# 64-row score tiles with the other head's queries zero, and a first group projected straight to padded form

## Chip, cores, metric

One core of a Trainium2 chip. The metric is the time of one launch on the device in microseconds (us). Time before the change: 1094.29 us, median of 3 runs (1092.95 to 1100.68). A trace's span, from first to last instruction, is some 2 to 7 us shorter than such a median.

PE is the matmul engine, PEld its weight load, ACT the scalar engine, DVE the vector engine, POOL and SP the other two; here SP mostly issues DMAs. "SPq" in a trace is SP's queue of instructions. The granted clock is the share of PE's full clock that the trace records: in these traces 1 or 0.5 at any moment (37 stretches of each in the trace before the change), and something between as a mean.

## The reference

Two branches over the same `x` (2048 x 512, bf16), mixed by a gate:

```python
g = sigmoid((x * gate_w).sum(-1, keepdims=True))
a = mha(x, wqkv, wo)          # 32 heads of width 16, softmax over 2048 keys
b = (silu(x @ w_gate) * (x @ w_up)) @ w_down      # F = 1792
return g * a + (1 - g) * b
```

Attention makes 32 x 2048 x 2048 scores, each of which needs an exponential. That is most of the work outside PE.

## The kernel before

The unit of work is a **slot**: one group of four heads (`g`), one block of 512 queries (`qb`), one tile of 128 keys (`kt`). There are 4 x 8 x 16 = 512 slots. In each, four score matmuls produce 128 x 512 scores each, and four PV matmuls (exponentials times values) consume their exponentials five slots later. Between them a pacer inserts pieces of all the other work (projections, gate, FFN, output projection), earliest deadline first. Each engine is given its instructions in program order, and in these traces an instruction that waits holds up those behind it on its engine: at a block boundary of the changed kernel DVE stood idle for 7.12 us before one reciprocal, then ran the next step, which had nothing left to wait for, right behind it.

A head is 16 wide, plus one row for a bound that keeps the exponent small. Each head is given a strip of 32 rows of the PE array:

```python
def score(ps, b):                       # b counts heads over all slots
    n, j = b // 4, b % 4
    ...
    mm(ps, lhsT=kaug[32 * j:32 * j + 32, g, kt * P:(kt + 1) * P],
       rhs=get_qaug(qb)[32 * j:32 * j + 32, g, :], start=True, stop=True, tile_position=(32 * j, 0))
```

Two heads at a time go to ACT (`act_pair`, `s_t` of 1024 columns, two PSUM buffers). Every eighth head (`on_vector`) goes to DVE, which computes its exponential with a polynomial in steps (score tile `d_t`, one PSUM buffer; below this is the "vector bank"):

```python
def on_vector(b):
    return b % 16 in (11, 15) and b < 4 * (SLOTS - 12)
```

Projected K and Q arrive with 16 rows per head; DMAs spread them to the strips, one DMA for each head:

```python
def spread_heads(t, b, src, c0, c1, first_on=None):
    for h in range(8):
        g, j = 2 * b + h // 4, h % 4
        eng = nc.sync if first_on is None or h % 2 == 0 else first_on
        eng.dma_start(out=t[32 * j + 1:32 * j + 1 + DH, g, c0:c1], in_=src[DH * h:DH * (h + 1), 0:c1 - c0])
```

The source of K is one of two staging tiles (`kst`). At the end of a query block the softmax denominators go out to DRAM and back; DVE inverts them, and they are broadcast (`rb`) for the output projection.

```python
def recip(qb, g1):
    ...
    nc.sync.dma_start(out=dn[0:4 * n, :], in_=dds[qb][0:n, :]. ...)
    def spread():
        recip16(rn[0:4 * n, :], dn[0:4 * n, :])          # DVE, in its program order
        ...                                               # to DRAM and broadcast to rb
    vops.append(spread)                                   # within the next slots
```

## Time and profile before

| | before |
|---|---|
| median of runs | 1094.29 us |
| span of the profiled run | 1087.0 us |
| mean granted TensorE clock | 0.833 |
| busy: PE, ACT, DVE | 81%, 81%, 74% |
| first exponential starts | 44.4 us |
| starts of exponentials 1 and 99 apart | 136.2 us |
| the next 782 exponentials | 860.2 us (1.100 each) |
| from there to the end | 46.2 us |

The last four rows come from the starts of the `e_t` instructions in the trace. They cut the span into parts that can be compared between kernels. The prediction below shows the profile's lines.

### The profile page before, as it was taken

How to read it: one execution, taken by the hardware profiler on the slowest of the kernel's cores; microseconds unless marked ns; L12 is line 12 of the kernel's file. 1: busy time of each engine (PE TensorE's matmuls, PEld its weight loads, DVE VectorE, ACT ScalarE, POOL GpSimd, SP SyncE). 2: the span in 40 equal slices, each digit the busy share in tenths (PEclk: the TensorE clock that was granted, in tenths of full speed). 3: DMA queues.
4: the chain of work that ended last, by engine and by line, in shares of the span. 5: the costliest groups of instructions: out<-in, count | busy, mean ns of one | idle time of the engine just before them, and what ended most of it. 6: DMA issues, size and time to landing. Idle time of an engine off the chain costs nothing.

```text
span 1087.0 us, 14674 instructions
## 1 busy us (share of the span) xinstructions
PE 875.1 (81%) x5109; PEld 208.7 (19%) x5109; DVE 807.2 (74%) x1475; ACT 883.2 (81%) x967; POOL 23.2 (2%) x25
## 2 busy tenths in 40 slices
PE   2796588988887888888887788988888788888874
PEld 0121122121221122122221121112221122222210
DVE  2387577787877788779777887778777787887833
ACT  0485577898987799889987898889897799999963
POOL 8000000000000000000000000000000000000000
PEclk9798665798987899689888897779895799889756
DMA  9000100111100001111001111110001011000000
GB/s 256 22 7 23 27 23 24 29 42 36 24 22 26 18 27 43 32 30 38 10 3 39 32 33 37 23 35 18 3 19 49 23 36 31 8 3 4 4 22 20
DMA packets 89774, 32.61 MB, mean 30 GB/s; under 512 B 75944, under 2 KB 89188, under 8 KB 89700
## 3 DMA queue, kind: packets, MB, share of 16 engines
q1 hardware_dynamic: 85012, 27.35, 10.3%
q10 hardware_dynamic: 4560, 4.26, 1.2%
q8 instruction: 40, 0.66, 0.2%
q14 instruction: 34, 0.28, 0.1%
q0 software_dynamic: 128, 0.07, 0.0%
HBM read 20.84 MB, written 2.35 MB: 21 GB/s over the span
## 4 chain that ended last, share of the span: by engine, by line
PE 35%; ACT 25%; DVE 18%; issue 13%; SPq 5%; DMA 3%; ACTq 0%; DVEq 0%
ACT e_t L171 24%; PE s_t L168 9%; PE o_ps L168 8%; DVE u_t L177 6%; DVE y_t L177 5%; PE d_t L168 4%; PE dps L168 4%; PE up L168 3%; PE gp L168 2%; SPq L255 2%; SPq L184 2%; DVE z_t L177 1%; ACT th L171 1%; DMA kaug<-kst 1%; PE a_ps L168 1%
## 5 line engine op out<-in xcount | busy, mean ns | idle before, releaser
L171 ACT ACTIVATE e_t<-s_t 128x1024 bf16<-128x1024 f32 x899 | 855.0, 1032 | 144.1 <-PE s_t L168 136.9
L168 PE MATMUL s_t<-qaug,kaug 32*128 32x512 bf16 x1798 | 371.5, 438 | 112.5 <-ACT e_t L171 108.5
L177 DVE TENSOR_SCALAR y_t<-d_t 128x512 uint16<-128x512 f32 x250 | 171.8, 687 | 115.9 <-PE s_t L168 96.2
L168 PE MATMUL o_ps<-e_t,vaug 128*32 128x512 bf16 x1798 | 231.1, 451 | 4.3 <-ACT e_t L171 4.3
L168 PEld LDWEIGHTS <-kaug 32*128 32x128 bf16 x2048 | 93.7, 93 | 500.5 <-issue 497.2
L177 DVE TENSOR_TENSOR u_t<-u_t,z_t 128x1024 f16<-128x1024 f16 x250 | 173.1, 693 | 8.6
L168 PE MATMUL d_t<-qaug,kaug 32*128 32x512 bf16 x250 | 110.1, 440 | 25.4 <-DVE y_t L177 25.0
L168 PE MATMUL o_ps<-y_t,vaug 128*32 128x512 bf16 x250 | 113.1, 452 | 2.6 <-DVE y_t L177 2.5
L177 DVE TENSOR_TENSOR y_t<-y_t,u_t 128x1024 uint16<-128x1024 uint16 x125 | 86.4, 692 | 4.3
L168 PE MATMUL gp<-xT,wg 128*128 128x512 bf16 x224 | 79.9, 444 | 3.1 <-DVE gs L177 3.1
L168 PE MATMUL up<-xT,wu 128*128 128x512 bf16 x224 | 81.6, 454 | 0.0
L168 PEld LDWEIGHTS <-vaug 128*32 128x32 bf16 x2048 | 51.7, 96 | 149.8 <-issue 149.8
L168 PE MATMUL dps<-wd_t,mt 128*128 128x512 bf16 x224 | 75.7, 428 | 0.0
L177 DVE TENSOR_SCALAR u_t<-z_t 128x1024 f16<-128x1024 uint16 x125 | 53.4, 427 | 4.3
L177 DVE TENSOR_SCALAR z_t<-y_t 128x1024 uint16<-128x1024 uint16 x125 | 53.3, 427 | 4.2
L177 DVE TENSOR_SCALAR y_t<-y_t 128x1024 uint16<-128x1024 uint16 x125 | 53.0, 424 | 2.7
L177 DVE TENSOR_SCALAR u_t<-u_t 128x1024 f16<-128x1024 f16 x125 | 52.7, 422 | 1.9
L177 DVE SCALAR_TENSOR_TENSOR mt<-gs,up 128x512 bf16<-128x512 bf16 x56 | 38.2, 683 | 18.4 <-PE up L168 18.2
L168 PE MATMUL kp<-xT,wqk 128*128 128x512 bf16 x64 | 23.6, 471 | 21.7 <-DMA xT<-in_A_x_dram 21.6
L177 DVE SCALAR_TENSOR_TENSOR gs<-th,gp 128x512 bf16<-128x512 bf16 x56 | 38.1, 680 | 1.5 <-ACT th L171 1.4
L171 ACT ACTIVATE th<-gp 128x512 bf16<-128x512 f32 x56 | 33.9, 605 | 4.5 <-PE gp L168 4.5
L168 PE MATMUL a_ps<-wo_t,on_qb 128*128 128x512 bf16 x64 | 24.8, 462 | 15.7 <-DVE on_qb L177 15.6
(57 smaller groups left out, 273.3 us busy)
## 6 DMA issues: line engine op xcount, KB each, us to landing
wg<-in_B_w_gate_dram SPq DMA_DIRECT2D x56, 128.0 KB
wu<-in_B_w_up_dram SPq DMA_DIRECT2D x56, 128.0 KB
out_dram<-o_t SPq DMA_DIRECT2D x16, 128.0 KB
qaug<-qst SPq DMA_DIRECT2D x124, 16.0 KB
on_qb<-osb SPq DMA_DIRECT2D x124, 16.0 KB
rb<-rr SPq DMA_DIRECT2D x15, 128.0 KB
wd_t<-in_B_w_down_dram ACTq DMA_DIRECT2D x1, 1792.0 KB
kaug<-kst SPq DMA_DIRECT2D x112, 16.0 KB
```

The source lines that it names most:

```text
L168: ordered(nc.tensor.matmul(*args, **kw))
L171: ordered(nc.scalar.activation(*args, **kw))
L177: return lambda *a, **kw: ordered(f(*a, **kw))
L184: nc.sync.dma_start_transpose(out=xT[:, dc, :], in_=x[:, dc * P:(dc + 1) * P])
L255: eng.dma_start(out=t[32 * j + 1:32 * j + 1 + DH, g, c0:c1], in_=src[DH * h:DH * (h + 1), 0:c1 - c0])
```

## The change

Intent: raise the part of the PE array that a score matmul uses, in the hope of a higher granted clock, and start the exponentials sooner. Two heads now share a 64-row tile; the queries of the other head are zero there, so its keys add nothing. Queries are therefore stored twice as wide (`j % 2`), in two buffers for two groups each instead of two for eight. The first group of the first block is projected with weights already padded to strips, which needs no spreading. Loads of `wo`, `w_down` and the gate move from the front to SP behind the transposes of `x`; all head DMAs are on SP; K and Q get new deadlines; each pair of groups has its own bound.

```diff
@@ score
+    HEADS = (0, 2, 1, 3)
     def score(ps, b):
-        n, j = b // 4, b % 4
+        n, j = b // 4, HEADS[b % 4]
-        mm(ps, lhsT=kaug[32 * j:32 * j + 32, g, kt * P:(kt + 1) * P],
-           rhs=get_qaug(qb)[32 * j:32 * j + 32, g, :], ..., tile_position=(32 * j, 0))
+        if qb == 0 and g == 0:
+            ...                                  # 32 rows of q0, the padded first group
+        else:
+            r = slice(64 * (j // 2), 64 * (j // 2) + 64)
+            mm(ps, lhsT=kaug[r, g, kt * P:(kt + 1) * P], rhs=get_qx(qb, g // 2)[r, j % 2, g % 2, :],
+               start=True, stop=True, tile_position=(64 * (j // 2), 0))
@@ on_vector
-        return b % 16 in (11, 15) and b < 4 * (SLOTS - 12)
+        return b % 16 in (10, 15) and 4 * KT <= b < 4 * (SLOTS - 12)
@@ start  (cut)
+    for dc in range(DC):                         # as each quarter of xT arrives
+        for tb in range(QB):
+            mm(kp0[...], lhsT=wpad[1][:, dc, :], rhs=xT[:, dc, ...], ...)
+        mm(qp0[:, :], lhsT=wpad[0][:, dc, :], rhs=xT[:, dc, 0:QBW], ...)
@@ spreading
-            eng = nc.sync if first_on is None or h % 2 == 0 else first_on
+                nc.sync.dma_start(...)           # all on SP; likewise qx<-qst
@@ pacing of K and Q  (cut)
-            prev = [pace.add(k_pieces(b, tb), 0, d - 12 + tb, prev)]
-        qs = [pace.add(q_pieces(qb, b), d - G * KT, d - 100 + 22 * b) for b in range(NB)]
+                    prev = [pace.add(k_pieces(b, tb), 0, d - (9 if first else 22) + tb, prev)]
+            q = pace.add(q_pieces(qb, b), 0 if first else max(0, d - 2 * KT + 1), d - (7 if first else 16))
```

More of the change, by code (lines that the diff above doesn't have):

```diff
@@ L185 @@
     wqk = big.tile([P, DC, 2 * D], BF16, name="wqk")
-    nc.scalar.dma_start(out=wqk[:], in_=A_wqkv[:, 0:2 * D].rearrange("(dc p) c -> p dc c", p=P))
+    for c0 in (0, D):
+        nc.scalar.dma_start(out=wqk[:, :, c0:c0 + 64],
+                            in_=A_wqkv[:, c0:c0 + 64].rearrange("(dc p) c -> p dc c", p=P))
+    for c0 in (0, D):
+        nc.scalar.dma_start(out=wqk[:, :, c0 + 64:c0 + D],
+                            in_=A_wqkv[:, c0 + 64:c0 + D].rearrange("(dc p) c -> p dc c", p=P))
     rb = big.tile([P, NB, QBW], BF16, name="rb")
@@ L191, with late_loads @@
     gw_col = const.tile([P, DC], BF16, name="gw_col")
-    nc.scalar.dma_start(out=gw_col[:], in_=gate_w.rearrange("(dc p) -> p dc", p=P))
     wo_t = big.tile([P, NB, D], BF16, name="wo_t")
-    nc.scalar.dma_start(out=wo_t[:], in_=A_wo.rearrange("(b p) d -> p b d", p=P))
     wo_l = big.tile([P, D], BF16, name="wo_l")
-    nc.gpsimd.memset(wo_l[:], 0.0)
-    for j in range(4):
-        nc.gpsimd.dma_start(out=wo_l[32 * j + 1:32 * j + 1 + DH, :],
-                            in_=A_wo[(H - 4 + j) * DH:(H - 3 + j) * DH, :])
-    wd_t = big.tile([P, FC, D], BF16, name="wd_t")
-    nc.scalar.dma_start(out=wd_t[:], in_=B_w_down.rearrange("(fc p) d -> p fc d", p=P))
-    kaug = big.tile([P, G, S], BF16, name="kaug")
-    for g in range(G):
-        (nc.vector if g < 2 else nc.gpsimd).memset(kaug[:, g, :], 1.0)
+    wd_t = big.tile([P, FC, D], BF16, name="wd_t")
+    def late_loads():
+        nc.sync.dma_start(out=gw_col[:], in_=gate_w.rearrange("(dc p) -> p dc", p=P))
+        nc.sync.dma_start(out=wo_t[:], in_=A_wo.rearrange("(b p) d -> p b d", p=P))
+        for j in range(4):
+            nc.sync.dma_start(out=wo_l[32 * j + 1:32 * j + 1 + DH, :],
+                              in_=A_wo[(H - 4 + j) * DH:(H - 3 + j) * DH, :])
+        nc.sync.dma_start(out=wd_t[:], in_=B_w_down.rearrange("(fc p) d -> p fc d", p=P))
+    kaug = big.tile([P, G, S], BF16, name="kaug")
+    wpad = [big.tile([P, DC, P], BF16, name=f"wpad{i}") for i in range(2)]
+    for i in range(2):
+        nc.vector.memset(wpad[i][:], 0.0)
+    onescol = const.tile([P, 1], F32, name="onescol")
+    nc.vector.memset(onescol[:], 0.0)
+    for j in range(4):
+        nc.vector.memset(onescol[32 * j:32 * j + 1, :], 1.0)
+    bsel0 = const.tile([P, P], BF16, name="bsel0")
+    nc.vector.memset(bsel0[:], 0.0)
+    for j in range(4):
+        nc.vector.memset(bsel0[32 * j:32 * j + 32, 32 * j:32 * j + 1], -1.0)
+    for i in range(2):
+        nc.vector.tensor_copy(
+            out=wpad[i][:, :, :].rearrange("p dc (j c) -> p dc j c", c=32)[:, :, :, 1:1 + DH],
+            in_=wqk[:, :, i * D:i * D + 64].rearrange("p dc (j c) -> p dc j c", c=DH))
+    for g in range(1, G):
+        nc.gpsimd.memset(kaug[:, g, :], 1.0)
     vaug = big.tile([P, KT, G * 4 * VC + 16], BF16, name="vaug")
@@ L215 @@
                    allow_small_or_imprecise_dtypes=True)
-    bsel = const.tile([P, NB, H], BF16, name="bsel")
-    lo_t = const.tile([P, H], F32, name="lo_t")
-    for b in range(NB):
-        for h in range(H):
-            c = 8 * (h % 4) + h // 4
-            if b == 0:
-                nc.vector.memset(lo_t[:, c:c + 1], float(DH * h))
-        ge_t = work.tile([P, H], F32, tag="ge_t", name="ge_t")
-        lt_t = work.tile([P, H], F32, tag="lt_t", name="lt_t")
-        nc.vector.tensor_scalar(out=ge_t[:], in0=lo_t[:], scalar1=pidx[:, 0:1], scalar2=float(P * b),
-                                op0=ALU.subtract, op1=ALU.subtract)
-        nc.vector.tensor_scalar(out=lt_t[:], in0=ge_t[:], scalar1=-float(DH) + 0.5, scalar2=-1.0,
-                                op0=ALU.is_gt, op1=ALU.mult)
-        nc.vector.scalar_tensor_tensor(out=bsel[:, b, :], in0=ge_t[:], scalar=0.5, in1=lt_t[:],
-                                       op0=ALU.is_lt, op1=ALU.mult)
+    bsel = const.tile([P, 8], BF16, name="bsel")
+    lo_t = const.tile([P, 8], F32, name="lo_t")
+    for h in range(8):
+        c = 2 * (h % 4) + h // 4
+        nc.gpsimd.memset(lo_t[:, c:c + 1], float(DH * h))
+    far_t = const.tile([P, 8], F32, name="far_t")
+    nc.vector.tensor_scalar(out=lo_t[:], in0=lo_t[:], scalar1=pidx[:, 0:1], scalar2=None, op0=ALU.subtract)
+    nc.vector.tensor_scalar(out=far_t[:], in0=lo_t[:], scalar1=-float(DH) + 0.5, scalar2=-1.0,
+                            op0=ALU.is_gt, op1=ALU.mult)
+    nc.vector.scalar_tensor_tensor(out=bsel[:, :], in0=lo_t[:], scalar=0.5, in1=far_t[:],
+                                   op0=ALU.is_lt, op1=ALU.mult)
+    nc.gpsimd.memset(wo_l[:], 0.0)
     sbc_t = const.tile([P, P], BF16, name="sbc_t")
@@ L238 @@
     kb = const.tile([P, NB], F32, name="kb")
-    kneg = const.tile([P, NB, H], BF16, name="kneg")
+    kneg = const.tile([P, NB, 8], BF16, name="kneg")
     gval = const.tile([P, KT], F32, name="gval")
@@ L248, with spread_heads @@
     kparts = {}
-    def spread_heads(t, b, src, c0, c1, first_on=None):
+    def spread_heads(t, b, src, c0, c1):
         for h in range(8):
             g, j = 2 * b + h // 4, h % 4
-            eng = nc.sync if first_on is None or h % 2 == 0 else first_on
-            eng.dma_start(out=t[32 * j + 1:32 * j + 1 + DH, g, c0:c1], in_=src[DH * h:DH * (h + 1), 0:c1 - c0])
+            if g > 0:
+                nc.sync.dma_start(out=t[32 * j + 1:32 * j + 1 + DH, g, c0:c1], in_=src[DH * h:DH * (h + 1), 0:c1 - c0])
     def k_pieces(b, tb, act_evac=False):
@@ L273, in f @@
                         vec.tensor_copy(out=seg, in_=st["p"][:, :])
-                    spread_heads(kaug, b, seg, tb * QBW, (tb + 1) * QBW, nc.scalar if b == 0 else None)
+                    spread_heads(kaug, b, seg, tb * QBW, (tb + 1) * QBW)
                     if tb == 0:
@@ L283, in k_bound @@
         vec.tensor_reduce(out=kb[:, b:b + 1], in_=kparts[b][:, :], axis=AX.X, op=ALU.max)
-        vec.tensor_scalar(out=kneg[:, b, :], in0=bsel[:, b, :], scalar1=kb[:, b:b + 1],
+        vec.tensor_scalar(out=kneg[:, b, :], in0=bsel[:, :], scalar1=kb[:, b:b + 1],
                           scalar2=None, op0=ALU.mult)
@@ L305, in v_pieces, with get_qx @@
         return [(2, pc(0)), (2, pc(1))]
-    qaugs = [big.tile([P, G, QBW], BF16, name=f"qaug{i}") for i in range(2)]
-    for t in qaugs:
+    qx = [big.tile([P, 2, 2, QBW], BF16, name=f"qx{i}") for i in range(2)]
+    for t in qx:
         nc.gpsimd.memset(t[:], 0.0)
+    q0 = big.tile([P, QBW], BF16, name="q0")
     aqs = {}
-    def get_qaug(qb):
-        return qaugs[qb % 2]
+    def get_qx(qb, b):
+        return qx[(qb * NB + b) % 2]
     def q_pieces(qb, b, act_evac=False):
@@ L331, in f @@
                         vec.tensor_copy(out=qst[:, :], in_=st["p"][:, :])
-                    qa = get_qaug(qb)
-                    spread_heads(qa, b, qst, 0, QBW, nc.scalar if act_evac else None)
+                    t = get_qx(qb, b)
+                    for hh in range(8):
+                        gg, j = hh // 4, hh % 4
+                        if (qb, b, gg) != (0, 0, 0):
+                            nc.sync.dma_start(out=t[32 * j + 1:32 * j + 1 + DH, j % 2, gg, :],
+                                              in_=qst[DH * hh:DH * (hh + 1), :])
                     aq = work.tile([P, QBW], BF16, tag="aq", name="aq", bufs=4)
@@ L339, in q_pieces, with bound_pieces @@
         return [(2, pc(0)), (2, pc(1))]
-    def bound_pieces(qb, b0, b1):
+    def bound_pieces(qb, b):
         def f():
             bp = ps_m.tile([P, QBW], F32, tag="m", name="bp")
-            for b in range(b0, b1):
-                mm(bp[0:H, :], lhsT=kneg[:, b, :], rhs=aqs[(qb, b)][:, :], start=(b == b0), stop=(b == b1 - 1))
-            bq = work.tile([H, QBW], BF16, tag="bq", name="bq")
-            vec.tensor_copy(out=bq[:, :], in_=bp[0:H, :])
-            qa = get_qaug(qb)
+            mm(bp[0:8, :], lhsT=kneg[:, b, :], rhs=aqs[(qb, b)][:, :], start=True, stop=True)
+            bq = work.tile([8, QBW], BF16, tag="bq", name="bq")
+            vec.tensor_copy(out=bq[:, :], in_=bp[0:8, :])
+            t = get_qx(qb, b)
             for j in range(4):
-                nc.sync.dma_start(out=qa[32 * j:32 * j + 1, 2 * b0:2 * b1, :],
-                                  in_=bq[8 * j + 2 * b0:8 * j + 2 * b1, :])
-        return [(b1 - b0, f)]
+                nc.sync.dma_start(out=t[32 * j:32 * j + 1, j % 2, :, :], in_=bq[2 * j:2 * j + 2, :])
+        return [(1, f)]
     def gate_pieces(t0):
@@ L430 @@
     unready = set()
+    HEADS = (0, 2, 1, 3)
     def score(ps, b):
-        n, j = b // 4, b % 4
+        n, j = b // 4, HEADS[b % 4]
         qb, g, kt = n // (G * KT), (n // KT) % G, n % KT
-        mm(ps, lhsT=kaug[32 * j:32 * j + 32, g, kt * P:(kt + 1) * P],
-           rhs=get_qaug(qb)[32 * j:32 * j + 32, g, :], start=True, stop=True, tile_position=(32 * j, 0))
+        if qb == 0 and g == 0:
+            r = slice(32 * j, 32 * j + 32)
+            mm(ps, lhsT=kaug[r, g, kt * P:(kt + 1) * P], rhs=q0[r, :], start=True, stop=True,
+               tile_position=(32 * j, 0))
+        else:
+            r = slice(64 * (j // 2), 64 * (j // 2) + 64)
+            mm(ps, lhsT=kaug[r, g, kt * P:(kt + 1) * P], rhs=get_qx(qb, g // 2)[r, j % 2, g % 2, :],
+               start=True, stop=True, tile_position=(64 * (j // 2), 0))
     def act_pair(bs):
@@ L488, in pv @@
             c0 = (4 * g + j) * VC
-            assert 4 * n + j not in unready
-            mm(o_of[un][32 * j:32 * j + 32, :], lhsT=vaug[:, kt, c0:c0 + 32], rhs=e_of.pop(4 * n + j),
+            b = 4 * n + HEADS.index(j)
+            assert b not in unready
+            mm(o_of[un][32 * j:32 * j + 32, :], lhsT=vaug[:, kt, c0:c0 + 32], rhs=e_of.pop(b),
                start=(kt == 0), stop=(kt == KT - 1), tile_position=(0, 32 * j), skip_group_check=True)
@@ L551, in f @@
                     if g1 < G and not acc:
-                        acc.append(get_qaug(qb - 1)[:, :, :].rearrange("p g c -> p (g c)").bitcast(F32)
-                                   .rearrange("p (t d) -> p t d", t=TQ))
+                        acc.append(big.tile([P, TQ, D], F32, name="acc"))
                 for b in (2 * i, 2 * i + 1):
@@ L570, in fin_pieces @@
         return [(2, pc(i)) for i in range(2)]
-    for tb in range(QB):
-        for _, f in k_pieces(0, tb, act_evac=(tb % 2 == 0)):
-            f()
-    for _, f in q_pieces(0, 0, act_evac=True):
-        f()
-    V0 = 4
-    for tt in range(2):
-        for _, f in v_pieces(tt, act_evac=True):
-            f()
-    k_bound(0)
-    for _, f in bound_pieces(0, 0, 1):
-        f()
-    for tt in range(2, V0):
+    kp0 = [ps_s.tile([P, 2 * QBW], F32, tag="s", name="kp0") for _ in range(2)]
+    qp0 = ps_m.tile([P, QBW], F32, tag="m", name="qp0")
+    for dc in range(DC):
+        for tb in range(QB):
+            mm(kp0[tb // 2][:, (tb % 2) * QBW:(tb % 2 + 1) * QBW], lhsT=wpad[1][:, dc, :],
+               rhs=xT[:, dc, tb * QBW:(tb + 1) * QBW], start=(dc == 0), stop=(dc == DC - 1))
+        mm(qp0[:, :], lhsT=wpad[0][:, dc, :], rhs=xT[:, dc, 0:QBW], start=(dc == 0), stop=(dc == DC - 1))
+    kpart0 = const.tile([P, 2], F32, name="kpart0")
+    act(out=kaug[:, 0, 0:2 * QBW], in_=kp0[0][:, :], func=ACT.Identity, bias=onescol[:, 0:1], scale=1.0)
+    vec.tensor_scalar(out=kaug[:, 0, 2 * QBW:4 * QBW], in0=kp0[1][:, :], scalar1=onescol[:, 0:1], scalar2=None,
+                      op0=ALU.add)
+    act(out=q0[:, :], in_=qp0[:, :], func=ACT.Copy)
+    vec.tensor_reduce(out=kpart0[:, 0:1], in_=kaug[:, 0, 2 * QBW:4 * QBW], axis=AX.X, op=ALU.max,
+                      apply_absolute_value=True)
+    vec.tensor_reduce(out=kpart0[:, 1:2], in_=kaug[:, 0, 0:2 * QBW], axis=AX.X, op=ALU.max,
+                      apply_absolute_value=True)
+    aq0 = work.tile([P, QBW], BF16, tag="aq", name="aq0", bufs=4)
+    vec.tensor_scalar(out=aq0[:, :].bitcast(U16), in0=q0[:, :].bitcast(U16), scalar1=0x7FFF, scalar2=None,
+                      op0=ALU.bitwise_and)
+    kb0 = const.tile([P, 1], F32, name="kb0")
+    kneg0 = const.tile([P, P], BF16, name="kneg0")
+    vec.tensor_reduce(out=kb0[:], in_=kpart0[:, :], axis=AX.X, op=ALU.max)
+    vec.tensor_scalar(out=kneg0[:], in0=bsel0[:], scalar1=kb0[:, 0:1], scalar2=None, op0=ALU.mult)
+    V0 = 5
+    for tt in range(V0):
+        if tt == 3:
+            bp0 = ps_d.tile([P, QBW], F32, tag="d", name="bp0")
+            mm(bp0[:, :], lhsT=kneg0[:, :], rhs=aq0[:, :], start=True, stop=True)
+            vec.tensor_tensor(out=q0[:, :], in0=q0[:, :], in1=bp0[:, :], op=ALU.add)
         for _, f in v_pieces(tt, act_evac=True):
@@ L595, with bnd @@
     prev = []
-    for b in range(1, NB):
-        d = 2 * b * KT
-        ks = []
-        for tb in range(QB):
-            prev = [pace.add(k_pieces(b, tb), 0, d - 12 + tb, prev)]
-            ks += prev
-        q = pace.add(q_pieces(0, b), 0, d - 7)
-        def bnd(b=b):
-            k_bound(b)
-        kbc = pace.add([(0.5, bnd)], 0, d - 7, ks)
-        prev = [kbc]
-        bc = pace.add(bound_pieces(0, b, b + 1), 0, d - 6, [q, kbc])
-        need.setdefault(d - 3, []).append(bc)
-    for qb in range(1, QB):
-        d = qb * G * KT
-        qs = [pace.add(q_pieces(qb, b), d - G * KT, d - 100 + 22 * b) for b in range(NB)]
-        bc = pace.add(bound_pieces(qb, 0, NB), d - G * KT, d - 10, qs)
-        need.setdefault(d - 4, []).append(bc)
-    gates = [pace.add(gate_pieces(4 * i), 0, 80 + 8 * i) for i in range(4)]
+    for qb in range(QB):
+        for b in range(NB):
+            d = (qb * G + 2 * b) * KT
+            first = qb == 0 and b == 0
+            if first:
+                d = KT
+            after = []
+            if qb == 0:
+                ks = []
+                for tb in range(QB):
+                    prev = [pace.add(k_pieces(b, tb), 0, d - (9 if first else 22) + tb, prev)]
+                    ks += prev
+                def bnd(b=b):
+                    k_bound(b)
+                after = prev = [pace.add([(0.2, bnd)], 0, d - (6 if first else 17), ks)]
+            q = pace.add(q_pieces(qb, b), 0 if first else max(0, d - 2 * KT + 1), d - (7 if first else 16))
+            bc = pace.add(bound_pieces(qb, b), 0 if first else max(0, d - 2 * KT + 1), d - (5 if first else 14), [q] + after)
+            need.setdefault(d - (4 if first else 6), []).append(bc)
+    gates = [pace.add(gate_pieces(4 * i), 40, 80 + 8 * i) for i in range(4)]
     gu = {(qb, fc): gu_chain(qb, fc) for qb in range(QB) for fc in range(FC)}
@@ L637 @@
             pcs = [(pcs[0][0], first)] + pcs[1:]
-            c = pace.add(pcs, 0, a0 + per * 0.6 * (fc + 1) / FC, prev)
+            c = pace.add(pcs, 24, a0 + per * (0.6 if qb < QB - 1 else 0.68) * (fc + 1) / FC, prev)
             prev = [c]
         for tq in range(TQ):
-            c = pace.add(down_pieces(qb, tq), 0, a0 + per * (0.6 + 0.3 * (tq + 1) / TQ), prev + fin_prev)
+            c = pace.add(down_pieces(qb, tq), 0, a0 + per * (0.6 + 0.3 * (tq + 1) / TQ if qb < QB - 1 else 0.68 + 0.32 * (tq + 1) / TQ), prev + fin_prev)
             prev = [c]
@@ L669 @@
             c.force()
+        if n == 8:
+            late_loads()
         pace.begin_slot(n)
```

## The prediction

> **What bounds the kernel now.** I read the page's slices first, then busy time by engine in stretches of 30 us, then the chain of waits, then the timeline of the start.
>
> ```profile
> span 1087.0 us, 14674 instructions
> ...
> PE 875.1 (81%) x5109; PEld 208.7 (19%) x5109; DVE 807.2 (74%) x1475; ACT 883.2 (81%) x967; POOL 23.2 (2%) x25
> ...
> PEclk9798665798987899689888897779895799889756
> ...
> L171 ACT ACTIVATE e_t<-s_t 128x1024 bf16<-128x1024 f32 x899 | 855.0, 1032 | 144.1 <-PE s_t L168 136.9
> L168 PE MATMUL s_t<-qaug,kaug 32*128 32x512 bf16 x1798 | 371.5, 438 | 112.5 <-ACT e_t L171 108.5
> ```
>
> No engine is full over the whole span: ACT (the exponentials e_t) and PE are both at 81%, and ACT's idle time is nearly all waiting for score tiles. The clock row is the odd one: the granted TensorE clock wanders between 0.5 and 1. Stretches of equal length show what it does (columns: stretch, length, PE, PEld, DVE, ACT, POOL busy with counts, clock, DMA share, GB/s):
>
> ```profile
> 480.00:510.00 30.00, 25.71 (x173) 6.82 (x171) 26.97 (x49) 29.80 (x35) 0.00 (x0) 1.00 0.15 34
> ...
> 660.00:690.00 30.00, 28.07 (x137) 5.31 (x136) 22.27 (x41) 24.75 (x28) 0.00 (x0) 0.61 0.13 30
> ...
> 1020.00:1050.00 30.00, 21.92 (x115) 4.46 (x114) 18.29 (x33) 23.97 (x26) 0.00 (x0) 0.53 0.06 19
> ```
>
> At clock 1.00 ACT is the bound (29.80 of 30 us, 35 instructions). At 0.61 PE is the bound (28.07 of 30) and only 28 get through. So the kernel alternates between two bounds, and the clock chooses.
>
> What chooses the clock? The trace's clock records have only the values 0.5 and 1, and every change falls on a grid of 3.413 us. I cut the matmul records of the trace on that grid and weighted each by the part of the array it uses: 1 for a 128x128 matmul, 1/4 for a score tile (32 rows), 1/4 for a PV tile (32 columns). If a window's sum was 6.5 or more, the next window ran at full clock in 145 of 146 cases; below 5 in 1 of 56; between, in about half. Plain busy time does not separate them (660 to 690 is 94% busy and slow). So what keeps the clock up is array area, not time. Mean sums per window: 7.5 in 480:510 (30 full, 70 score, 72 PV matmuls in 30 us), 5.9 in 660:690, 4.0 where attention runs alone (1020 to 1040). Attention tiles alone can't hold the clock; interleaved FFN matmuls do.
>
> Pace, from the starts of the 782 exponentials between 180 and 1040 us: 0.999 us each at full clock (607.6 us / 608), 1.451 at half clock (252.4 / 174). ACT's own floor at full clock is 0.917 from exponential to exponential plus 0.478 for each of 56 tanh, so 0.917 + 0.030 = 0.947.
>
> The start:
>
> ```profile
> 12.55 0.59 PE L168 MATMUL kp<-xT,wqk 128*128 128x512 bf16 x1 [12.55 <-DMA xT<-in_A_x_dram]
> ...
> 23.31 1.01 PE L168 MATMUL kp<-xT,wqk 128*128 128x512 bf16 x2 [1.50 <-DMA xT<-in_A_x_dram]
> ```
>
> The last quarter of xT arrives at 23.3, the first exponential starts at 44.4: 21 us of projections, copies, spreading DMAs and the bound. Between 45 and 180 us only 98 exponentials run in 135 us, with the chain naming kaug spreads and the bound's vector work.
>
> [...] The trace shows 32-row tiles used mostly in pairs: two take 0.39 us at full clock, four 0.60. [...] xT crawled (about 140 KB per 2 us) while the weight loads ran, then moved 430 to 470 KB per 2 us.
>
> **The change part by part.**
> 1. 64-row score tiles. Every score tile outside the first group of the first query block doubles its area, 1/4 to 1/2, at the same 512 columns. Work isn't added in time: 32-row and full matmuls last alike in the groups (438 ns against 454 for up). The sum of 480:510 becomes 7.5 + 70/4 * 3.413/30 = 9.4; attention alone at ACT's pace (about 8.4 scores and 8.4 PV per window) becomes 4.2 + 2.1 = 6.3, in the band that mostly holds; with any FFN matmul it is above. Of 112 windows at half clock, 70 would reach 6.5 with scores at 1/2 even before they speed up. So the clock stays near 1 between about 50 us and the last FFN work. The tail of FFN is also stretched to slot 500 to cover the end.
> 2. Pairs are reordered to heads (0,2),(1,3), so a pair still sits in two different row halves and overlaps. What is lost is four-way overlap, and d_t beside a pair: about 0.21 us for each of 242 d_t tiles, 51 us of PE over the span. PE at full clock is 25.7 of 30, so it becomes about 27.3: still under ACT.
> 3. Vector engine takes 242 score tiles instead of 250. ACT gets 4 exponentials more (+3.7 us). DVE loses 8 * 2.58 = 21 us (0.687 + half of the seven-step chain of 3.78), 6 us of set-up, and gains about 8 us of copies of smaller bounds: 807 to about 788.
> 4. wo and w_down (2.3 MB) leave the first 23 us: at the 236 GB/s of the first 30 us that is 10 us of transfer, of which I count 7.5: last xT at about 16. Then 5 cold matmuls (2.1), a copy of 1024 columns (1.2), two maxima (2.4), the small bound steps (0.7), the bound's matmul and addition (1.3) and V projections beside them: first exponential at about 28 instead of 44.4. The spreading DMAs and their waits fall out for group 0.
> 5. K and Q of the next groups get earlier deadlines (22 slots ahead instead of 12), gates and FFN wait till slots 40 and 24. In the first 16 slots 84 full matmuls (0.27 each in pairs of 0.54, 22.7 us) join 16 * 0.97 us of attention: 38 us for 32 exponentials; then 66 at 1.05 make 69. Together 107 instead of 136.
>
> Sum: first exponential 28, first 98 exponentials 107, then 903 - 98 - 19 = 786 at 0.99 (between floor and the measured full-clock pace, nearer to the latter) = 778, the last stretch 47 as before (19 exponentials, with its wait for the denominators' round trip through DRAM). 960 us as a profiled span; times the ratio of median to span, 1094.3/1087.0, 966 us.
>
> **The rivals.**
> - [...] For it: half of each moving tile is zero, and no run yet has shown how zeros count. Against it: nothing in the records separates windows better than area. Then the clock stays near 0.83 and only parts 4 and 5 pay: about 1050.
> - PE becomes the bound through lost overlap (part 2) [...]
> - DVE becomes the bound. 788 us of work against about 900 us from first exponential to last is 87%; in 480:510 it already runs at 90% beside a full ACT, so it fits, but with little room; a pace of 1.03 gives about 1000.
> - The start stalls: all spreading DMAs are now on one queue (0.59 us per issue), and only two staging buffers for K exist. Some 10 to 15 us.
>
> **Range and chances.** The central sum is 966. A pace near the floor (0.955) takes 27 us off and a shorter tail a few more: 932. Half clock in a sixth of the steady part (131 exponentials * 0.45 = 59 us) or a DVE-bound pace brings about 1005. Even the first rival is faster by over 2%. Faster 0.97, within 2% 0.02, slower 0.01.
>
> **What would show it.** Clock row near 1 from slice 2 to the last but two; mean clock above 0.93 (now 0.833). ACT's idle time before e_t down from 144 to about 60 us; pace per exponential 0.95 to 1.0. First exponential between 26 and 32 us. Score matmuls at full clock still about 0.39 us. The prediction is wrong if the clock still drops during FFN stretches (area idea false), or if it stays at 1 and ACT still waits over 100 us for s_t (PE or DVE the new bound).

Its sum: 28 + 107 + 778 + 47 = 960 us as a span, 966 us as a median. The rivals: the first was that rows of zeros might not count for the clock, or that it follows something other than area. The second also had a part about weight loads, with a cost that is not in the sum. Of part 4's items: in the trace before, the first projections ("cold", until 28 us, where the clock records begin) start 0.43 us apart when they follow one another, those at full clock 0.22; the other items are estimates from the operations in it. The changed kernel's trace then had 1.11 and 1.28 us for the copies of 1024 columns and 2.35 for the two maxima.

## The result

1043.07 us, median of 4 runs (1041.19 to 1045.07), against 1097.49 us for the kernel before on the same chip (median of 4). The ratio is 0.9507, with a 95% interval of 0.9459 to 0.9556. Ratios are the mean time of one kernel's fast runs over that of the other's of the same rounds, so not quite the ratio of the medians. The direction was right, but of the forecast gain (1094 to 966 us) more than half is missing.

The page of the changed kernel, the lines that answer to those shown of the kernel before:

```profile
span 1040.3 us, 14644 instructions
...
PE 829.7 (80%) x5042; PEld 219.0 (21%) x5130; DVE 794.7 (76%) x1428; ACT 885.0 (85%) x971; POOL 19.9 (2%) x30
...
PEclk9978869999989999999998899999998999999977
...
L171 ACT ACTIVATE e_t<-s_t 128x1024 bf16<-128x1024 f32 x903 | 858.4, 1036 | 120.6 <-PE s_t L168 112.2
L168 PE MATMUL s_t<-qx,kaug 64*128 64x512 bf16 x1742 | 383.5, 396 | 107.3 <-ACT e_t L171 100.9
```

The clock did rise, to a mean of 0.938. But ACT's idle time before exponentials fell only from 144 to 121 us. Set against the prediction's own sum:

| part of the span | before | predicted | after |
|---|---|---|---|
| to the first exponential | 44.4 | 28 | 24.6 |
| first 98 exponentials | 136.2 | 107 | 126.3 |
| the middle | 860.2 | 778 | 845.5 |
| last 19 and the end | 46.2 | 47 | 43.9 |

The first exponential came even sooner than forecast. The first 98 are 19 us over, and the middle is 67.5 us over. Three places in the trace show where.

**An extra pass on PE.** In the kernel before, at full clock, a vector-bank score starts together with a pair (columns: start, us, engine, line, operation, tiles):

```profile
493.82 0.39 PE L168 MATMUL d_t<-qaug,kaug 32*128 32x512 bf16 x1
493.82 0.39 PE L168 MATMUL s_t<-qaug,kaug 32*128 32x512 bf16 x2
...
494.14 0.40 PE L168 MATMUL o_ps<-e_t,vaug 128*32 128x512 bf16 x3
```

In the changed kernel it doesn't:

```profile
608.03 0.39 PE L168 MATMUL d_t<-qx,kaug 64*128 64x512 bf16 x1
608.25 0.39 PE L168 MATMUL s_t<-qx,kaug 64*128 64x512 bf16 x2
...
608.57 0.40 PE L168 MATMUL o_ps<-e_t,vaug 128*32 128x512 bf16 x3
```

From d_t to the next PV it takes 0.54 us instead of 0.32: three 32-row tiles ran side by side there, three 64-row tiles don't here. Over the whole trace, at full clock, an unbroken run of three scores takes a median of 0.39 us before (147 runs) and 0.60 us now (154).

**A queue at the start.** The changed kernel at about 90 us (brackets: how long the engine had been idle, and what ended it):

```profile
86.21 31.05 SPq L274 DMA_DIRECT2D kaug<-kst  x48
...
92.59 0.69 DVE L177 CAST kst<-kp 128x512 bf16<-128x512 f32 x1 [2.64 <-DMA kaug<-kst]
...
94.39 0.58 PE L168 MATMUL o_ps<-y_t,vaug 128*32 128x512 bf16 x1 [4.30 <-DVE y_t L177]
...
97.03 1.02 ACT L171 ACTIVATE e_t<-s_t 128x1024 bf16<-128x1024 f32 x1 [5.87 <-PE s_t L168]
```

SP issues 48 spreading DMAs in 31 us, almost without a gap. DVE wants to copy the next K and waits for a staging tile that SP has not yet sent off; behind that copy in DVE's order stands the last step of an exponential; PE waits for that, and ACT for PE. This queue isn't new: in the kernel before, SP issued almost without a gap from 74 to 150 us (twice 32 spreading DMAs of K in some 20 us each), and DVE waited 13.5 us for staging tiles; now it waits 15.6 us.

**A queue at the block boundaries.** At the end of the first query block:

```profile
295.42 3.12 SPq L357 DMA_DIRECT2D qx<-qst  x5
...
298.63 2.50 SPq L375 DMA_DIRECT2D qx<-bq  x4
...
301.24 0.53 SPq L538 DMA_DIRECT2D dd<-osb  x1
...
304.68 0.52 SPq L551 DMA_DIRECT2D dn<-dd  x1
...
306.71 0.95 DVE L177 RECIPROCAL rn<-dn 128x128 bf16<-128x128 bf16 x1 [7.12 <-DMA dn<-dd]
...
309.36 1.02 ACT L171 ACTIVATE e_t<-s_t 128x1024 bf16<-128x1024 f32 x1 [8.24 <-PE s_t L168]
```

The denominators (`dd`) have to wait on SP until the next queries have been spread. Meanwhile the reciprocal stands at the head of DVE, and ACT is idle for 8.24 us. Such gaps come again at 553 us (6.2) and 795 us (4.5). In the kernel before, the four waits of DVE for `dn` added up to 10.7 us; now they are 19.1:

```profile
DVE rn L177 <- DMA dn<-dd: 10.7, 4, 3.1
```

```profile
DVE rn L177 <- DMA dn<-dd: 19.1, 4, 7.1
```

(Columns: total us, times, longest.)

### The profile page after: what moved, and what is told of

Read it like the earlier page. It is cut to its first block, busy times and chain, and to the rows that moved or that the text cites. A ratio compares the mean times of both kernels' runs of the same rounds, so it can differ in the third digit from the quotient of the medians.

```text
span 1040.3 us, 14644 instructions
## 1 busy us (share of the span) xinstructions
PE 829.7 (80%) x5042; PEld 219.0 (21%) x5130; DVE 794.7 (76%) x1428; ACT 885.0 (85%) x971; POOL 19.9 (2%) x30
## 3 DMA queue, kind: packets, MB, share of 16 engines
HBM read 20.84 MB, written 2.35 MB: 22 GB/s over the span
## 4 chain that ended last, share of the span: by engine, by line
PE 34%; ACT 25%; DVE 18%; issue 13%; SPq 5%; DMA 4%; DVEq 0%; ACTq 0%
ACT e_t L171 24%; PE s_t L168 11%; PE o_ps L168 7%; DVE y_t L177 6%; DVE u_t L177 5%; PE d_t L168 4%; PE dps L168 4%; PE gp L168 2%; SPq L274 2%; ACT th L171 2%; PE a_ps L168 1%; DVE z_t L177 1%; PE up L168 1%; PE vp L168 1%; DVE osb L177 1%
## 5 line engine op out<-in xcount | busy, mean ns | idle before, releaser
L171 ACT ACTIVATE e_t<-s_t 128x1024 bf16<-128x1024 f32 x903 | 858.4, 1036 | 120.6 <-PE s_t L168 112.2
L168 PE MATMUL s_t<-qx,kaug 64*128 64x512 bf16 x1742 | 383.5, 396 | 107.3 <-ACT e_t L171 100.9
L168 PE MATMUL o_ps<-e_t,vaug 128*32 128x512 bf16 x1806 | 214.3, 406 | 4.1 <-ACT e_t L171 3.6
L168 PEld LDWEIGHTS <-kaug 64*128 64x128 bf16 (+1 forms) x2048 | 103.7, 94 | 481.7 <-issue 475.3
L168 PE MATMUL d_t<-qx,kaug 64*128 64x512 bf16 x242 | 96.7, 400 | 21.1 <-DVE y_t L177 19.5
L168 PE MATMUL o_ps<-y_t,vaug 128*32 128x512 bf16 x242 | 98.1, 405 | 7.6 <-DVE y_t L177 7.6
L168 PE MATMUL gp<-xT,wg 128*128 128x512 bf16 x201 | 65.0, 397 | 6.7 <-DVE gs L177 3.6
L168 PE MATMUL up<-xT,wu 128*128 128x512 bf16 x202 | 63.2, 389 | 2.5 <-issue 2.4
L168 PE MATMUL dps<-wd_t,mt 128*128 128x512 bf16 x200 | 62.6, 390 | 2.9 <-issue 2.9
L168 PE MATMUL a_ps<-wo_t,on_qb 128*128 128x512 bf16 (+1 forms) x57 | 21.5, 442 | 16.8 <-DVE on_qb L177 15.9
L177 DVE CAST kst<-kp 128x512 bf16<-128x512 f32 x16 | 11.0, 689 | 21.8 <-DMA kaug<-kst 15.6
```

Source lines behind the costliest of these rows:

```text
L168: ordered(nc.tensor.matmul(*args, **kw))
L171: ordered(nc.scalar.activation(*args, **kw))
L177: return lambda *a, **kw: ordered(f(*a, **kw))
```

## The experiments

All ten gave the right result. Except where it says otherwise, each is the changed kernel (1043.07) with one edit. In the first four the kernel before, run on the same chip, had a median of 1093.61 us; in the other six 1093.61 us too, on another chip (one run stands in both lists). Of the runs of the kernel before on the second chip, which spread from 1081 to 1098 us, the record calls three slow and leaves them out of the ratios. The gains and losses below are against the changed kernel, whose chip the record doesn't name; e7, which turned out to be the same program, gave 1042.44 us on the second chip.

### e1: score tiles back to 32 rows

```diff
-            r = slice(64 * (j // 2), 64 * (j // 2) + 64)
+            r = slice(32 * j, 32 * j + 32)
             mm(ps, lhsT=kaug[r, g, ...], rhs=get_qx(qb, g // 2)[r, j % 2, g % 2, :],
-               start=True, stop=True, tile_position=(64 * (j // 2), 0))
+               start=True, stop=True, tile_position=(32 * j, 0))
```

> The changed kernel with only its score tiles back at 32 rows (same padded queries, same head order, same pacing), so what is left is the new start and pacing. Theory C (the forecast's: a half clock itself costs 0.45 us per exponential): mean clock back to about 0.83, a quarter of the 903 exponentials at the half-clock pace, so about 1043 + 90 = 1130 us. Theory S (selection: the stalls make the low-clock windows, the clock itself costs little, because ACT is the bound or waits on something else): clock about 0.83 all the same, but only 1055 to 1080 us.

Measured: 1088.81 us (1082.12 to 1094.19), clock 0.819. Ratio to the kernel before 0.9962 (0.9905 to 1.0018): the same. It lies between the two expectations. The 64 rows are worth 46 us net. The new start and pacing, though they begin exponentials 19 us sooner, are worth nothing clear of the noise at the end: the middle takes 884.7 us, 24.5 more than before, of which 4 more exponentials are some 4.

### e2: the extra pass doubled

```diff
         score(d_t[:, :], b)
+        score(d_t[:, :], b)
```

> Each of the 242 vector-bank scores d_t is computed twice (same result), which doubles the extra pass that 64-row tiles cost beside a pair (0.22 us at full clock, 53 us of PE in all). If PE has slack under ACT, as the forecast said: less than 6 us slower, under 1049. If PE's in-order stream is on the path: 25 to 55 us slower, 1068 to 1098; then the lost overlap of the change itself cost about as much.

Measured: 1069.85 us (1069.29 to 1074.81), clock 0.941: 27 us slower. ACT's waits for scores rise, first the changed kernel, then this one (columns: total us, times, longest):

```profile
ACT e_t L171 <- PE s_t L168: 112.2, 131, 8.2
```

```profile
ACT e_t L171 <- PE s_t L168: 144.5, 201, 9.1
```

They rise in number, from 131 to 201, not in length. So 53 us of PE work (242 x 0.22) cost 27 us of time, although PE is "only" 80% busy. The likely reason is the order: what PE does between two pairs can delay the next pair, and ACT holds only two score buffers.

### e3: half of the head DMAs on POOL's queue

```diff
-                nc.sync.dma_start(out=t[32 * j + 1:32 * j + 1 + DH, g, c0:c1], ...)
+                (nc.sync if h % 2 == 0 else nc.gpsimd).dma_start(out=t[...], ...)   # likewise for qx<-qst
```

> Half of the head-spreading DMAs (kaug<-kst and qx<-qst) are issued from the POOL queue instead of SP. If SP's issue time (0.63 us each, over 130 of them before 125 us) bounds the first 98 exponentials through the two K staging buffers and the in-order vector engine: they take 105 to 112 us instead of 126, and the boundary waits shrink too, total 1010 to 1028. If the landing or the vector work is the bound, or POOL issues more slowly: within 5 us of 1043 or slower.

Measured: 1023.94 us (1023.34 to 1024.12): 19 us faster. The first 98 exponentials take 111.8 us instead of 126.3, and the middle falls from 845.5 to 840.9. DVE's waits for K's staging tiles, 15.6 us in the changed kernel, are gone. So the issue time of one queue bounded the start (in the changed kernel SP issued 48 spreading DMAs in 31.05 us, 0.65 us each). At the block boundaries the cure is partial: DVE still waits 14.4 us for `dn` instead of 19.1, and the gaps are 5.9, 4.7 and 4.3 us.

### e4: the reciprocal later

```diff
-        vops.append(spread)
+        if qb < QB - 1:
+            held.append(spread)          # taken up 9 slots later
+        else:
+            vops.append(spread)
...
-            rel = (qb + 1) * G * KT + LAG + 14 if not last else SLOTS - 8
+            rel = (qb + 1) * G * KT + LAG + 22 if not last else SLOTS - 8
```

> At the three query-block boundaries the reciprocal that waits in order on VectorE for the denominators' round trip is issued 9 slots later, and the output projection 8 slots later. If that in-order wait makes the 8.2, 6.2 and 4.5 us stalls of ACT at 309, 553 and 795 us and the 3 to 4 us ones after them: they go, 15 to 25 us faster, 1018 to 1028. If the stall is due to something else (scores waiting for queries): no change.

Measured: 1028.59 us (1024.69 to 1031.15): 14.5 us faster, just short of the 15 to 25 that were expected. The gaps of 8.2, 6.2 and 4.5 us are gone from ACT; in the middle the largest left is 3.7 us.

### e5: both

The edits of e3 and e4 together.

> POOL queue and late reciprocal together in the changed kernel. Alone they gave 19 and 14.5 us. If they cure separate waits (the start's staging buffers; the boundaries' in-order reciprocal): 1043 - 33 = 1010 us, 1006 to 1015. If both cured the same queueing of DMAs on SP at the boundaries: 1018 to 1024.

Measured: 1010.82 us (1008.22 to 1015.32): 32 us faster than the changed kernel, the sum of 19 and 14.5. They are separate waits.

### e6: 32 rows beside the vector bank

```diff
-        if qb == 0 and g == 0:
+        if qb == 0 and g == 0 or b % 16 in (0, 1, 10, 11, 12, 15):
+            rhs = q0 if qb == 0 and g == 0 else get_qx(qb, g // 2)[:, j % 2, g % 2, :]
             r = slice(32 * j, 32 * j + 32)
```

> The changed kernel with 32-row tiles again only for the vector-bank scores d_t and the pair next to each (6 of 16 scores), 64 rows for the other 10. If the extra pass beside d_t is the 27 us that doubling it cost, and the clock needs only the area (10/2 + 6/4 = 6.5 per 16 scores instead of 8, against 4 before): clock stays above 0.92 and the time falls by 15 to 27 us, 1016 to 1028. If switching between 32- and 64-row tiling costs as much, or the clock falls: 1040 or slower.

Measured: 1034.7 us (1034.13 to 1036.17), clock 0.923: 8 us faster, less than expected. The overlap is back where the trace shows such a triple: DVE's wait for d_t is again put down mostly to s_t, 74.9 us, and to d_t 19.5, as in the kernel before. But the clock is lower by 0.015, which may cost too: some 10 us by the line of 6.4 us per 0.01 below, an estimate from a correlation. What the switching between 32 and 64 rows costs, if anything, was not separated.

### e7: the bound's matmul one slot later

```diff
-        return slot >= self.release and all(a.done() for a in self.after)
+        return slot >= self.release and all(a.done() and slot >= a.done_at + self.gap for a in self.after)
...
+            bc.gap = 1
```

> The changed kernel with each bound's matmul held one slot after its Q projection, so that PE does not stand in order behind VectorE's absolute value of Q (13.7 us of PE idle in 10 waits, new with the change, which has 15 bounds where there were 7). If these waits reach the end time: 1031 to 1037 us. If they are swallowed by ACT's queue of score tiles: within 4 us of 1043.

Measured: 1042.44 us (1039.78 to 1044.36): no change. But the edit had no effect: in the two traces every engine has the same instructions in the same order, and PE's wait for `aq` is still 13.7 us in 10 places, the longest 4.3. So this is a repeat of the changed kernel, and what that wait costs was not tested. (The trace has 17 bound matmuls, not 15.)

### e8: 64 rows alone, in the kernel before

The **kernel before** with 64-row tiles in query blocks 1 and 3 only (one of its two query buffers is wide), heads in the new order and vector places 10 and 15. Four scratch tiles that only DVE uses, or that are used once, got one buffer instead of two to make room.

```diff
-    qaugs = [big.tile([P, G, QBW], ...) for i in range(2)]
+    qaugs = [big.tile([P, 1 + i, G, QBW], ...) for i in range(2)]
...
+        if qb % 2 == 0:
+            ...                                            # 32 rows as before
+        else:
+            r = slice(64 * (j // 2), 64 * (j // 2) + 64)   # rhs from plane j % 2
```

> The kernel before with 64-row score tiles alone, and only in query blocks 1 and 3 [...]; blocks 0 and 2 keep 32 rows; vector-bank scores at places 10 and 15. If the 64 rows act through the clock by themselves: clock near 1 in blocks 1 and 3, each 9 to 15 us shorter than in the kernel before, blocks 0 and 2 unchanged, 1065 to 1078 in all. If they only pay together with the new pacing: within 6 us of 1094.

Measured: 1059.52 us (1057.65 to 1069.6; the profiled run is the slowest of them), ratio 0.9765 (0.9661 to 0.9869). Each block is a stretch of its own in one trace (columns: stretch, length, then PE, PEld, DVE, ACT, POOL, clock, DMA share, GB/s). This kernel, blocks 1 (64 rows), 2 (32 rows) and 3 (64 rows):

```profile
320.00:557.00 237.00, 198.30 (x1237) 52.39 (x1256) 195.92 (x349) 217.84 (x238) 0.00 (x0) 0.97 0.10 26
557.00:804.00 247.00, 204.24 (x1227) 50.48 (x1246) 197.12 (x351) 218.50 (x241) 0.00 (x0) 0.87 0.11 26
804.00:1052.00 248.00, 195.37 (x1206) 50.75 (x1225) 183.41 (x324) 218.88 (x239) 0.00 (x0) 0.93 0.08 20
```

The kernel before, the same three blocks:

```profile
320.00:569.00 249.00, 210.08 (x1265) 50.18 (x1262) 197.00 (x349) 218.67 (x239) 0.00 (x0) 0.87 0.10 25
569.00:815.00 246.00, 207.79 (x1246) 49.78 (x1244) 196.71 (x350) 218.53 (x240) 0.00 (x0) 0.86 0.11 27
815.00:1071.00 256.00, 209.03 (x1229) 48.28 (x1227) 183.88 (x324) 219.90 (x240) 0.00 (x0) 0.81 0.07 19
```

By the starts of their exponentials block 1 is 11 us shorter (237.2 against 248.2), at clock 0.97, and block 3 is 8 us shorter (248.6 against 256.6), at 0.93; block 2, which has the new head order and vector places but 32 rows, stays at 0.87 and is not shorter. The tile height works by itself, without the new start or pacing. (The median lies below the 1065 to 1078 us expected.)

### e9: all three cures

The edits of e3, e4 and e6 together.

> All three cures: half the head DMAs on POOL, the late reciprocal, and 32-row tiles beside the vector bank. If the 8 us of the mixed tiles add to the 32 us of the other two: 1000 to 1005 us, the best so far. If the mixed tiles only bought time inside the stalls: 1008 to 1012.

Measured: 1001.36 us (996.97 to 1004.75), ratio 0.9207 (0.9127 to 0.9286). The gains add up. It is the fastest of all, 42 us below the changed kernel. ACT waits 73.4 us for scores in 92 places.

### e10: both cures, 32 rows everywhere

The edits of e1, e3 and e4 together.

> POOL queue and late reciprocal with all score tiles at 32 rows: what the 64-row tiles are worth once those waits are gone. If the clock's worth is independent of the waits: 46 us as between the changed kernel and its 32-row form, 1052 to 1062, clock about 0.83. If the 64 rows mainly covered for the stalls (low clock after a stall): the clock without them is above 0.87 and the difference under 30 us, below 1040.

Measured: 1068.33 us (1060.46 to 1073.65), clock 0.812 in the profiled run. That is slower than either expectation. Against e5 the 64 rows are worth 57 us, more than with the waits in place. So the low clock was no mere shadow of these stalls: take them away, and it is as low as before and costs as much.

## Why the prediction was right or wrong, point by point

**Array area holds the clock: right.** The forecast was above 0.93; 0.938 was measured. In e1 the 32-row form of the same kernel went back to 0.819. In this kernel, then, zero rows count. Cut on the same 3.413 us grid (all 73 changes of the clock in the trace before the change, and all 31 after it, lie on it to within 0.01 us) with 64-row tiles at 1/2, windows of the changed kernel with a sum of 6.5 or more led to full clock in 248 of 249 cases, those between 4 and 6.5 in 13 of 32, much as before the change (54 of 129). Were the zero rows left out (weight 1/4), 108 of 116 windows between 4 and 6.5 would have led to full clock, which doesn't fit. The first rival (zero rows don't count) falls. (The trace has 5042 matmul records beside 5130 weight loads, so the sums are up to 2% low.)

**What the clock is worth: about as forecast, before deductions, as far as a correlation tells.** The prediction had 82 us in the middle (860 - 778), pace and clock together. A second measure: the 15 timed runs of the unchanged kernel for which a clock is recorded differ by themselves, from 0.815 (1098.49 us) to 0.842 (1081.06 us). A line through them falls by 6.4 us per 0.01 of clock (correlation -0.96); without the three called slow it is 6.2. That is a correlation and no experiment. If it carries over, e1 to the changed kernel (mean clock of the runs 0.819 to 0.940) should give 78 us and gave 46; e10 to e5 (0.821 to 0.958) should give 88 and gave 57. Both lack about 31 us, and the doubled pass of e2 cost 27.

**"Still under ACT" (part 2): the step that failed first.** The prediction sized the lost overlap rightly as 51 us of PE and then charged nothing, because PE's busy time stayed below ACT's. The runs show 27 us for as much again (e2). That the first such pass cost as much as the second is an inference, but the traces of the middle agree, each exponential counted by the clock at its start: the pace at full clock is 0.999 us in the kernel before and in e10 and 1.011 in e1, all with 32 rows, but 1.041 in the changed kernel (790.3 us / 759) and 1.035 in e5, with 64 rows. From e1 to the changed kernel and from e10 to e5 that makes an estimate of 23 and 28 us. The prediction had named the sign itself: a clock near 1, and ACT still waiting over 100 us for scores (112.2). The lost overlap was even among the rivals, as a PE that becomes the bound. But an engine need not be the bound for its work to count. In program order a pass in front of a score pair can make ACT wait, and a busy share of 80% hides that. e6 gave back 8 us of it, with a lower clock.

**107 us for the first 98 exponentials (part 5): 126 measured.** The prediction counted PE and ACT work and left SP's issue time to a rival of "10 to 15 us". e3 takes 14.5 us off this part and lands at 111.8. The removed waits for group 0 were real, but the queue that was full before stayed full: group 1 lost its share of ACT's queue, and the later groups' DMAs, on SP all along, came 48 in a row. (Part 4 held: its items add up to 23.7 us, not 28; the rest was reserve that wasn't needed, and 24.6 was measured.)

**0.99 us per exponential in the middle: 1.076 measured.** It was read from stretches that ran at full clock and then used for the whole middle. Of the 67.5 us over, 39 lie at full clock, at 1.041 instead of 0.99, for the most part the lost overlap above. The other 29 lie in half-clock windows: 27 exponentials in 55.3 us. The forecast of a nearly steady full clock left these out. In the kernel before, between 180 and 1040 us, ACT idled 24.5 of the 607.6 us at full clock, but 72.5 of the 252.4 at half clock (a wait counted where it ends), and nearly all gaps above 2 us (22.7 of 25.2 us) ended in the latter. A stalled PE has little area in its window, and a stall often comes first: in the changed kernel's middle all eight gaps above 2 us began at full clock, and in five of them the clock fell 0.7 to 2.5 us later. So part of the "half-clock pace" was stalls, which more area doesn't cure. It was not most of it: e10 has 13.8 us of such gaps instead of e1's 34.5, and its half-clock pace is still 1.454. In the middle of the changed kernel these gaps come to 33.7 us, more than before, and to as much in e1, so they belong to the pacing and not to the 64 rows. One reason is on SP at 295 us: Q of the next block's second pair may be spread only from the first slot after the boundary on, just when the denominators go out. The prediction took the new deadlines for an easing and did not see that a query buffer of two groups ties the spreading to the boundary. e4 shows the part of it that the in-order reciprocal makes: 14.5 us.

**The sum.** On spans the forecast missed 80 us: -3 at the first exponential, +19 in the first 98, +67 in the middle, -3 at the end. e5 cures 32 us, and the lost overlap is some 27 by e2, which makes some 59. The other 20 or so were not split by an experiment. e9 is still 42 us above the forecast in the middle (1.043 against 0.99); ACT idles there 33 us at full clock and 22 at half clock, and no run tells which of it could go. The prediction's upper end was also added up wrongly: its 59 us of half clock on 966 make 1025, not 1005.

**The other rivals.** DVE as the bound: it is 76% busy, nothing in the runs needs it as the cause, and no run tested it alone. Weight loads: no run tested them, and the traces show no loss: four scores in an unbroken run, two pairs, take a median of 0.76 us at full clock (63 runs) against 0.80 before (47). PE's new wait for `aq`, 13.7 us: not tested either, since e7 changed nothing.

## What to carry to other kernels

If the clock follows array area, as here (64 rows with zeros instead of 32: mean clock 0.819 to 0.938), padding small matmuls with zeros can buy clock, but price the side-by-side execution it gives up (here 0.22 us for each vector-bank score): count the passes in program order between two feeds of the bounding engine, not its busy share. Do not read the value of a state only from the windows in which the kernel happened to be in it; a stall can come before a state (here the clock fell after five of eight gaps had begun), so take a stall away, or the state, and run. Look in the trace whether an edit removed the wait that it was meant to remove (e7 did not). When work moves earlier or into a smaller buffer, list what else its DMA queue must issue at that time.
